# Zero fills on a DMA-bound kernel: 64 rows of 16 KB in place of 128 rows of 8 KB

## Chip, cores, metric

One core of a Trainium2 chip runs the whole program. The metric is the device time of one execution in microseconds; medians of several runs are quoted, with the lowest and highest. The time before is 646.59 us (646.42 to 647.03, 3 runs).

## The reference, cut to what matters

The program is the forward and backward pass of one decoder step for a single token: adaptive layer norm, attention over the last 4096 entries of a 65,536-entry cache, a gated feed-forward block, and the gradients of all inputs. What matters here is the size of two of those gradients:

```python
k = jnp.repeat(k_cache[:, :, Sk - W:, :], rep, axis=1)     # W = 4096 of Sk = 65536
v = jnp.repeat(v_cache[:, :, Sk - W:, :], rep, axis=1)
...
_out, _vjp = jax.vjp(_f, A_x, A_k_cache, A_v_cache, A_wq, A_wo, ...)
_grads = _vjp(grad_out)        # the gradients of k_cache and v_cache have the caches' shape
```

Only the last 4096 entries of each cache are read, so 15/16 of these two gradients (126 MB of bf16) is zero and has to be written all the same.

## The kernel before

The zeros are written to HBM, the chip's main memory, by 120 DMAs of 1 MiB ("fills") from one tile of zeros, 128 rows (partitions) of SBUF, the on-chip memory. They are filler: tuned lists say how many are issued after which step, so that the DMA engines always have work. Fills issued by GpSimd read bf16 zeros and write them as float32, so half as many bytes are read as are written ("widening"); the zeros that land are the same. Fills issued by ScalarE, in the feed-forward stage, read as much as they write.

```python
ZW = 4096
zeros = vt([P, ZW], "zeros", BF16)                     # 128 rows of 8 KB
nc.vector.memset(zeros.bitcast(U32), 0)
zregions = []
for og in (out_2, out_3):                              # gradients of k_cache, v_cache
    for g in range(G):
        region = og[0, g, 0:SKW, :].rearrange("r d -> (r d)").rearrange("(p x) -> p x", p=P)
        for i in range(region.shape[1] // ZW):
            zregions.append(region[:, i * ZW:(i + 1) * ZW])     # 128 rows of 8 KB, 120 KiB apart
zleft = list(zregions)
zeros8 = zeros[:, 0:ZW // 2]                           # 4 KB of each of the 128 rows

def zero(n, after=None, q=None):
    for _ in range(n):
        if not zleft:
            return
        if q is None:
            ins = nc.gpsimd.dma_start(out=zleft.pop(0).bitcast(FP32), in_=zeros8[:, :])   # widening
        else:
            ins = q.dma_start(out=zleft.pop(0), in_=zeros[:, :])
        ...
```

Three queues feed the same 16 DMA engines. GpSimd's queue (q0 in the profile) carries the 61 widening fills, 54 stores of gradients, and 14 loads of the feed-forward stage; SyncE's (q1) carries nearly all other loads and 7 large stores; ScalarE's (q10) carries the other 59 fills. Of the 61, 29 are issued before the feed-forward stage, among loads only. The last 32 come after it, and there the same queue carries stores.

```python
outer_dve(wq_t[j], h1[:, j:j + 1], dq_b)
nc.gpsimd.dma_start(out=dwq_view[:, j, :], in_=wq_t[j])    # a plain store: reads all 128 rows
zero(Z_DWQ[i])                                             # widening fills, same queue
```

Of the kernel before, what the change touches and what calls it, by code (L numbers as in the profile page):

```python
# [10 lines left out]
P = 128  # L11
FP32 = mybir.dt.float32
# [14 lines left out]
DH = 128  # L27
# [28 lines left out]
def kernel(  # L56
# [26 lines left out]
    nc = tc.nc  # L83
    SKW = A_k_cache.shape[2] - W
# [15 lines left out]
    def vt(shape, name, dt=FP32):  # L100
        return pool.tile(shape, dt, name=name)
# [4 lines left out]
    ZW = 4096  # L106
    zeros = vt([P, ZW], "zeros", BF16)
# [11 lines left out]
    zregions = []  # L119
    for og in (out_2, out_3):  # L120
        for g in range(G):
            region = og[0, g, 0:SKW, :].rearrange("r d -> (r d)").rearrange("(p x) -> p x", p=P)
            for i in range(region.shape[1] // ZW):
                zregions.append(region[:, i * ZW:(i + 1) * ZW])
    zleft = list(zregions)
    zeros8 = zeros[:, 0:ZW // 2]

    def dep(later, earlier):
        tc.add_manual_dep(later.ins, earlier.ins.name,
                          mybir.DependencyInfo(mybir.DependencyClass.Sync, mybir.DependencyReason.DATA),  # L130
                          reason="pace")

    def zero(n, after=None, q=None):
        for _ in range(n):
            if not zleft:
                return
            if q is None:
                ins = nc.gpsimd.dma_start(out=zleft.pop(0).bitcast(FP32), in_=zeros8[:, :])  # L138
            else:
                ins = q.dma_start(out=zleft.pop(0), in_=zeros[:, :])  # L140
            if after is not None:
                dep(ins, after)

# [104 lines left out]
    for j in range(KD):  # L248
        nc.sync.dma_start(out=wq_t[j], in_=wq_view[:, j, :])

    zero(Z_INIT)

    tp0 = ptp.tile([P, 24], BF16, name="tp_rows", tag="tp")
# [26 lines left out]
    for j in range(KD):  # L280
        for k in range(KM):
            mm = nc.tensor.matmul(mod_ps[:, k:k + 1], lhsT=wm_t[j][:, k * P:(k + 1) * P],
                                  rhs=cs_bf[:, j:j + 1], start=(j == 0 and k == 0), stop=(j == KD - 1),
                                  skip_group_check=True)
        if j < KD - 1:
            make_w01(j)
        zero(Z_MOD[j], mm)
# [25 lines left out]
    for j in range(KD):  # L313
        for h in range(HQ):
            mm = nc.tensor.matmul(q_ps[:, h:h + 1], lhsT=wq_t[j][:, h * P:(h + 1) * P],  # L315
                                  rhs=h1_bf[:, j:j + 1], start=(j == 0 and h == 0), stop=(j == KD - 1),
                                  skip_group_check=True)
        zero(Z_Q[j], mm)
# [429 lines left out]
```

## Time and profile before

| | before |
|---|---|
| median of 3 runs | 646.59 us |
| profiled span | 643.5 us |
| HBM read, written | 76.55 MB, 185.60 MB |
| GpSimd fills | 61, 7808 packets of 8 KB |

The page of a profile has a row of DMA shares (tenths, one digit for each fortieth of the span), a row of GB/s for the same slices, and a line for each queue (packets, MB, share of the 16 engines' time). The prediction below shows these lines of the kernel before. One more view of it is needed later, the windows of the closing stage, where stores and fills share q0. Its columns are the stretch and its length, busy time (and instructions) of each engine, the granted TensorE clock, the DMA share, and the GB/s moved.

```profile
core 0: us, PE busy (x) PEld busy (x) DVE busy (x) ACT busy (x) POOL busy (x), PEclk, DMA share, GB/s
492.00:544.00 52.00, 0.00 (x0) 0.00 (x0) 25.91 (x13) 0.00 (x0) 6.28 (x12) 0.50 1.10 425
544.00:634.00 90.00, 25.61 (x200) 20.41 (x199) 73.01 (x72) 33.75 (x56) 19.64 (x35) 0.50 1.07 423
```

The DMA share, 1.10 and 1.07, is over 1: the times of the packets overlap. In both stretches the engines move 423 to 425 GB/s, the plateau of this kernel.

### The profile page before, as it was taken

Reading aid. Unit: us, or ns where it says so; the run is one execution under the profiler, and the core shown is the slowest. Engines: PE = TensorE matmul, PEld = TensorE weight load, DVE = VectorE, ACT = ScalarE, POOL = GpSimd, SP = SyncE. Lnnn points to the kernel's source line nnn. Section 1 sums busy time; section 2 is a strip of 40 time slices with the busy share of each in tenths; the row PEclk is TensorE's granted clock in tenths of the full one; section 3 lists DMA queues with packets and bytes.
Section 4 is the critical chain, followed back from the end, with each engine's and each line's share of the span. In section 5 each row is a group of like instructions: output and inputs, shape, how many; then the busy total and the mean of one; then the engine's idle time right before and its main releaser. Section 6 shows DMA issues by size and latency. Waiting matters only on the chain.

```text
span 643.5 us, 7106 instructions
## 1 busy us (share of the span) xinstructions
PE 149.8 (23%) x2784; PEld 127.3 (20%) x2784; DVE 319.7 (50%) x626; ACT 206.8 (32%) x306; POOL 83.0 (13%) x137
## 2 busy tenths in 40 slices
PE   3122227562302020020201102310680000424300
PEld 2122215462301020010101101210460000423200
DVE  3442005600844518064180914899800079997194
ACT  2000016610531412543024432789670000425800
POOL 2000000040010100102001010212111012212211
PEclk9999999855555555555555555565755555555555
DMA  9999999999999999999999999999999999999996
GB/s 348 421 425 420 421 420 416 402 411 398 410 422 422 420 414 400 410 398 406 413 368 401 409 416 418 394 382 425 422 423 427 423 424 426 428 426 416 425 426 250
DMA packets 43810, 262.63 MB, mean 408 GB/s; under 512 B 4096, under 2 KB 4096, under 8 KB 18432
## 3 DMA queue, kind: packets, MB, share of 16 engines
q0 software_dynamic: 23184, 131.08, 51.5%
q1 hardware_dynamic: 12048, 69.22, 29.0%
q10 hardware_dynamic: 8544, 61.88, 23.8%
q8 instruction: 22, 0.36, 0.2%
q14 instruction: 12, 0.10, 0.0%
HBM read 76.55 MB, written 185.60 MB: 407 GB/s over the span
## 4 chain that ended last, share of the span: by engine, by line
DMA 64%; DVE 14%; ACT 11%; PE 5%; issue 4%; POOL 1%; SPq 0%; POOLq 0%; ACTq 0%; DVEq 0%
DMA out_dram<-arena 26%; DMA arena<-in_B_w_gate_dram 15%; DVE arena L172 7%; DMA arena<-in_w_mod_dram 7%; DMA arena<-in_A_wq_dram 6%; ACT arena L176 5%; DMA arena<-in_A_k_cache_dram 5%; DMA out_dram<-zeros 4%; DVE junk L172 2%; PE tp_kv L346 2%; DVE arena L168 1%; ACT arena L349 1%; ACT arena L234 1%; PE gu_ps L480 1%; ACT du_b L512 1%
## 5 line engine op out<-in xcount | busy, mean ns | idle before, releaser
L172 DVE CUSTOM_DVE_ANT_0 arena<-arena 128x4096 bf16<-128x4096 bf16 (+1 forms) x24 | 80.1, 3352 | 51.3 <-DMA arena<-in_w_mod_dram 51.3
L480 PE MATMUL gu_ps<-h_bf,arena 128*128 128x1 bf16 x448 | 16.8, 172 | 186.2 <-DMA arena<-in_B_w_up_dram 122.1
L155 DVE TENSOR_TENSOR hh<-sg,gu_ps 128x4 f32<-128x4 f32 x7 | 1.1, 158 | 113.8 <-ACT om L485 113.8
L138 POOL DMA_DIRECT2D out_dram<-zeros x61 | 33.7, 557 | 183.1 <-PE q_ps L315 49.5
L480 PEld LDWEIGHTS <-arena 128*128 128x128 bf16 x448 | 16.2, 118 | 187.9 <-issue 138.7
L653 PEld LDWEIGHTS <-arena 8*128 8x128 bf16 x256 | 25.9, 131 | 102.8 <-issue 99.2
L176 ACT ACTIVATE arena<-du_b,h 128x512 bf16<-128x512 bf16 x56 | 35.2, 711 | 33.8 <-DMA arena<-in_B_w_down_dram 31.3
L176 ACT ACTIVATE arena<-dg_b,h 128x512 bf16<-128x512 bf16 x56 | 35.3, 707 | 25.6 <-DMA out_dram<-zeros 12.7
L349 ACT COPY arena<-tp_kv 128x1024 bf16<-128x1024 bf16 x13 | 13.1, 1010 | 89.6 <-PE tp_kv L346 89.6
L657 ACT CAST arena<-ps_kv 128x512 bf16<-128x512 f32 x32 | 16.1, 691 | 75.1 <-DMA out_dram<-arena 75.1
L172 DVE CUSTOM_DVE_ANT_0 junk<-arena,b1k 128x1024 bf16<-128x1024 bf16 x28 | 34.2, 1223 | 8.2 <-DMA arena<-in_B_w_down_dram 7.7
L172 DVE CUSTOM_DVE_ANT_0 arena<-arena,b1k 128x1024 bf16<-128x1024 bf16 x32 | 36.7, 1218 | 0.4 <-ACT b1k L234 0.4
L172 DVE CUSTOM_DVE_ANT_0 arena<-arena,du_b 128x512 bf16<-128x512 bf16 x56 | 34.9, 686 | 3.5 <-ACT du_b L512 3.5
L172 DVE CUSTOM_DVE_ANT_0 arena<-arena,dg_b 128x512 bf16<-128x512 bf16 x56 | 34.8, 684 | 0.0
L653 PE MATMUL ps_kv<-DO_hd,arena 8*128 8x128 bf16 x128 | 15.9, 296 | 75.1 <-ACT arena L657 75.1
L176 ACT ACTIVATE arena<-b1k,o_col 128x1024 bf16<-128x1024 bf16 x32 | 33.4, 1137 | 0.0
L164 DVE COPY arena<-tp_kv 128x1024 bf16<-128x1024 bf16 x19 | 12.9, 690 | 27.3 <-PE tp_kv L346 27.2
L346 PE MATMUL tp_kv<-ident_bf,arena 128*128 128x128 bf16 x256 | 21.3, 246 | 20.7 <-DMA arena<-in_A_k_cache_dram 12.6
L484 ACT ACTIVATE sg<-gu_ps 128x4 f32<-128x4 f32 x7 | 1.2, 174 | 73.6 <-PE gu_ps L480 73.6
L433 POOL DMA_DIRECT2D arena<-in_B_w_up_dram x7 | 6.2, 891 | 131.3 <-DMA out_dram<-arena 102.3
L659 ACT ACTIVATE arena<-ps_kv 128x512 bf16<-128x512 f32 x32 | 16.1, 624 | 21.6 <-DMA out_dram<-arena 21.6
L346 PEld LDWEIGHTS <-arena 128*128 128x128 bf16 x256 | 18.4, 111 | 23.6 <-DMA arena<-in_A_k_cache_dram 13.5
(185 smaller groups left out, 377.5 us busy)
## 6 DMA issues: line engine op xcount, KB each, us to landing
out_dram<-zeros POOLq DMA_DIRECT2D x61, 1024.0 KB, 20.9
out_dram<-zeros ACTq DMA_DIRECT2D x59, 1024.0 KB, 21.4
out_dram<-arena POOLq DMA_DIRECT2D x46, 1024.0 KB, 20.2
arena<-in_A_wq_dram SPq DMA_DIRECT2D x16, 1024.0 KB, 20.7
arena<-in_w_mod_dram SPq DMA_DIRECT2D x8, 1536.0 KB, 30.8
arena<-in_A_wo_dram SPq DMA_DIRECT2D x8, 1024.0 KB, 23.7
arena<-in_w_mod_dram SPq DMA_DIRECT2D x8, 1024.0 KB, 27.3
arena<-in_B_w_down_dram SPq DMA_DIRECT2D x7, 1024.0 KB, 11.8
```

Of the source, the lines that this page charges most:

```text
L138: ins = nc.gpsimd.dma_start(out=zleft.pop(0).bitcast(FP32), in_=zeros8[:, :])
L164: return nc.vector.tensor_copy(out=out, in_=a)
L168: return nc.vector.tensor_scalar(out=out, in0=a, scalar1=s1, scalar2=None, op0=op0)
L172: return nc.vector.tensor_tensor_reduce(out=out, in0=w, in1=b, scale=1.0, scalar=0.0, op0=ALU.mult, op1=ALU.add, accum_out=acc)
L176: return nc.scalar.activation(out=out, in_=b, func=ACT.Copy, scale=col)
L234: last = nc.scalar.copy(out=o, in_=ps[:, :])
L346: nc.tensor.transpose(tp[:, t8 * P:(t8 + 1) * P], src[:, g, t_ * DH:(t_ + 1) * DH], ident_bf[:, :])
L349: last = nc.scalar.copy(out=o, in_=tp[:, :])
L480: nc.tensor.matmul(gu[:, half * 4 + jj:half * 4 + jj + 1], lhsT=w[:, j, jj::4], rhs=h2_bf[:, j:j + 1], start=(j == 0), stop=(j == KD - 1))
L653: nc.tensor.matmul(ps[:, t4 * DH:(t4 + 1) * DH], lhsT=rows[32 * g:32 * g + HG, t_ * P:(t_ + 1) * P], rhs=hd[32 * g:32 * g + HG, :], start= ...
L657: nc.scalar.copy(out=o, in_=ps[:, :])
L659: nc.scalar.activation(out=o, in_=ps[:, :], func=ACT.Copy, scale=float(scale))
```

## The change

The intent is to halve the number of packets of the widening fills: 64 rows of 16 KB written in place of 128 rows of 8 KB. For that each fill region becomes one contiguous MiB (for ScalarE's fills too, which keep 128 rows of 8 KB).

```diff
-            region = og[0, g, 0:SKW, :].rearrange("r d -> (r d)").rearrange("(p x) -> p x", p=P)
-            for i in range(region.shape[1] // ZW):
-                zregions.append(region[:, i * ZW:(i + 1) * ZW])
+            region = og[0, g, 0:SKW, :].rearrange("r d -> (r d)")
+            for i in range(SKW * DH // (P * ZW)):
+                zregions.append(region[i * P * ZW:(i + 1) * P * ZW])
 zleft = list(zregions)
-zeros8 = zeros[:, 0:ZW // 2]
+zeros8 = zeros[0:64, :]
 ...
-                ins = nc.gpsimd.dma_start(out=zleft.pop(0).bitcast(FP32), in_=zeros8[:, :])
+                ins = nc.gpsimd.dma_start(out=zleft.pop(0).rearrange("(p x) -> p x", p=64).bitcast(FP32), in_=zeros8[:, :])
             else:
-                ins = q.dma_start(out=zleft.pop(0), in_=zeros[:, :])
+                ins = q.dma_start(out=zleft.pop(0).rearrange("(p x) -> p x", p=P), in_=zeros[:, :])
```

So the change has three parts: the packets (16 KB), the addresses in HBM (contiguous), and the rows of SBUF that are read (0 to 63 only).

## The prediction

> **What bounds the kernel now.** I read the page first: the span, the row of DMA shares, the queues and the chain that ended last.
>
> ```profile
> span 643.5 us, 7106 instructions
> ...
> DMA  9999999999999999999999999999999999999996
> GB/s 348 421 425 420 421 420 416 402 411 398 410 422 422 420 414 400 410 398 406 413 368 401 409 416 418 394 382 425 422 423 427 423 424 426 428 426 416 425 426 250
> DMA packets 43810, 262.63 MB, mean 408 GB/s; under 512 B 4096, under 2 KB 4096, under 8 KB 18432
> ...
> q0 software_dynamic: 23184, 131.08, 51.5%
> q1 hardware_dynamic: 12048, 69.22, 29.0%
> q10 hardware_dynamic: 8544, 61.88, 23.8%
> ...
> DMA 64%; DVE 14%; ACT 11%; PE 5%; issue 4%; POOL 1%; SPq 0%; POOLq 0%; ACTq 0%; DVEq 0%
> ```
>
> The DMA engines are 90% busy or more in 39 of 40 slices; no compute engine passes 50%. The kernel is bound by DMA throughput: 262 MB at a plateau of about 427 GB/s would take 614 us, so only some 30 us are lost, at the head, in the middle stage with 1 KB rows, and at the tail. The chain agrees: 64% DMA. Queue q0 is what GpSimd issues (widening fills, its stores and some loads), q1 is SyncE, q10 is ScalarE. The list of DMA issues says what the change can touch:
>
> ```profile
> out_dram<-zeros POOLq DMA_DIRECT2D x61, 1024.0 KB, 20.9
> out_dram<-zeros ACTq DMA_DIRECT2D x59, 1024.0 KB, 21.4
> ```
>
> There are 120 fills of 1 MiB, nearly half of all bytes. The 61 from GpSimd read bf16 and write float32, so each reads half of what it writes; the 59 from ScalarE do not widen. A fill takes 21 us to land because it waits behind others, not because it is slow.
>
> Then I asked for the rate in stretches where the trace's DMA packets have one size or one mixture:
>
> ```profile
> core 0: us, PE busy (x) PEld busy (x) DVE busy (x) ACT busy (x) POOL busy (x), PEclk, DMA share, GB/s
> 20.00:30.00 10.00, 2.87 (x96) 2.71 (x96) 4.87 (x4) 0.00 (x0) 0.53 (x1) 1.00 1.07 420
> 124.00:150.00 26.00, 14.57 (x416) 13.85 (x415) 4.17 (x10) 4.38 (x6) 6.97 (x11) 0.63 1.13 410
> 168.00:176.00 8.00, 2.15 (x44) 1.99 (x41) 7.32 (x25) 4.96 (x7) 0.00 (x0) 0.50 1.12 427
> 630.00:633.00 3.00, 0.00 (x0) 0.00 (x0) 3.00 (x6) 0.00 (x0) 1.05 (x2) 0.50 1.02 411
> ```
>
> The last column is what matters. At 168 to 176 us nearly all packets are fills of 8 KB: 427 GB/s. At 630 to 633 all are plain stores of 4 KB: 411. At 20 to 30 the fills alternate with 12 KB weight loads: 420.
>
> Last I read the late part of the chain, because the wait there opens the closing stretch:
>
> ```profile
> 471.93 26.83 DMA out_dram<-arena
> 498.76 0.02 SPq L602
> ...
> 499.23 18.68 DMA arena<-in_w_mod_dram
> 517.92 0.02 issue
> 517.94 4.42 DVE arena L172
> ```
>
> VectorE has nothing to do from 467 to 518 us: it waits for a load on q1 that could start only when a store on q0 had landed. Both share the engines with fills.
>
> [...]With 12 KB loads on q1, the 8 KB fills of q0 carry about 40% of the bytes (8 of 20); with 2 KB loads (124 to 150 us) 78 to 80% (8 of 10); with 8 KB loads (503 to 518 us) 46 to 54%. [...]plain packets last 84 ns for 2 KB, 159 for 4 KB, 309 for 8 KB, so about 9 ns are fixed. The widening fills mostly last 322 alone and 341 when packets overlap; the 427 GB/s above corresponds to one per 307 ns per engine. [...]Here contiguous stores of 8 KB a row (gradients of k, v and wq) run at 426 to 428 in the late stage; 16 KB a row is not seen before.
>
> **The change part by part.**
>
> *Packets.* Each of the 61 widening fills becomes 64 packets of 16 KB: 7808 packets become 3904. From the windows: a 4 KB packet costs 4096 x 16 / 411 = 159.5 ns of an engine, an 8 KB packet 8192 x 16 / 427 = 307.0 ns. On a straight line through both, 16 KB cost 602 ns against 614 for two of 8 KB. Saved: 12 ns x 3904 / 16 engines = 2.9 us. That is an upper estimate: beside another queue part of the gap is probably already covered, and the 12 KB loads, at 420 to 422, are not faster than the 8 KB ones. I take 2 us.
>
> *Issue.* GpSimd spends 532 ns to issue a fill[...]. Nothing on the path.
>
> *Instructions.* No order changes: the comparison of the two programs finds the same rows on PE, VectorE, ScalarE and SyncE, and on GpSimd only the fills' shape differs.
>
> *Addresses.* All fills, ScalarE's too, now cover a contiguous 1 MiB instead of rows at a pitch of 120 KiB. Contiguous stores already reach 427, as the old pitch does: I count 0, with 2 us either way for the middle stage, where fills stand beside stores of 1 KB rows and the rate dips to about 330 for a few us at a time.
>
> *Shares.* [...]Fills are filler, and loads on q1 are waited for. In the first 100 us the fills are paced by matmuls that wait for these loads, so about one more fill gets ahead of a load, and the total before any point stays nearly the same. At 499 to 518 us q0 moved about half of 18.7 us x 424 GB/s, some 4 MB, and went on until about 526 us with another 1.2 MB. With 67% it would get those before the load lands: 1.2 / 0.424 = 2.8 us later. Against it, the store that lands at 498.8 waits behind fills on its own queue, which now drain faster. Net 0 to 2.8 us; I take 1.5 us lost.
>
> *Sum.* -2 + 1.5 + 0 = -0.5 us: 646.59 becomes about 646.
>
> **Rivals.**
>
> [...]A fill must read 512 KiB. [...]Against it: fills mostly alternate with loads, which read no SBUF[...]. Only at 166 to 176, 497 to 502 and in parts of 430 to 440 and 590 to 615 us does q0 run alone. I expect 0 to 4 us.
>
> *Fewer engines.* If 64 rows landed on 8 engines only, those would carry 8 MB of fills each and 12.4 MB of the rest: 20.4 MB at 26.7 GB/s per engine is 764 us. [...]
>
> *Better packets than thought.* If the widening itself costs a fixed 13 ns (322 against 309) that is now paid once for 16 KB, another 3 us go: 641 us. Overlap of packets (DMA share 1.12) speaks against it: that latency is already hidden.
>
> *Contiguity helps the middle stage.* If the dips there came from the fills' pitch, up to 8 us could go: 638 us. The dips come when the 1 KB-row stores end, so I think them theirs.
>
> **Range and chances.** The terms are all small beside 2% (13 us), and partly cancel. Centre 646 us. Low end 639: both kinder rivals in part. High end 657[...]. Under 633.7 would need an effect that I can't name: 4%. Above 659.5[...]: 14%. Within 2%: 82%.
>
> **What would show each step.** Queue q0 should have about 3900 packets fewer and the same bytes; its 16 KB packets should last 620 to 650 ns. [...]fills with double landing time and a DMA share near one half on average, fewer engines. The share step shows in the bytes of q0 against q1 at 10 to 30 and 503 to 518 us, and in when the w_mod load that VectorE waits for lands (517.9 us before). Addresses show on q10 alone: its 8 KB packets at 309 to 313 ns and the dips in the middle stage. The prediction is wrong if [...]small shifts of loads open idle stretches in the closing 120 us.

Passages of the prediction that say something of the hardware which no trace or run of this case shows are cut, and marked. -2 us (packets) + 1.5 (shares) + 0 (addresses) came to -0.5 us, 646 us. The 67% under "Shares" is the author's estimate from the shares of bytes in the trace before: where 8 KB fills stood beside 12 KB loads they had 40% (8 of 20), beside 8 KB loads 46 to 54%, so 16 KB fills beside 8 KB loads were given 16 of 24. The first rival: that the reads of SBUF from rows 0 to 63 become the bound. Its 0 to 4 us, and with it the high end of 657 us and the 14% for over 659.5, were estimates, shown by no trace.

Numbers of the trace before for what the prediction says without them: GpSimd's 129 transfers all land in the order of their issue, and its fills 20.9 us after it in the median, where 1 MiB at 427 GB/s takes 2.46 us, so a fill waits behind others. Before fills of the first 100 us GpSimd sat idle for 49.5 and 22.6 us until matmuls (into q_ps and mod_ps) had ended. The dip to about 330 is 331 GB/s at 334 to 342 us, after a store of 1 KB rows landed at 333.7.

## The result, and the profile after

The changed kernel takes 667.93 us (666.96 to 680.47, 3 runs; the slowest counts as a slow run, one over 1.5% above the fastest). Ratios in this document are the mean time of one kernel's fast runs over the mean of the other's fast runs of the same rounds, so they are not quite the ratio of the medians; here it is 1.032, with a 95% interval of 1.029 to 1.035. The prediction's range ended at 657.

The page of the changed kernel, for the lines shown of before:

```profile
span 666.2 us, 7106 instructions
...
GB/s 347 424 424 426 420 426 411 413 410 395 417 414 407 418 416 331 422 411 408 396 372 419 355 419 404 371 403 382 412 419 419 427 403 393 377 409 328 355 380 186
DMA packets 39906, 262.63 MB, mean 394 GB/s; under 512 B 4096, under 2 KB 4096, under 8 KB 18432
...
q0 software_dynamic: 19280, 131.08, 50.4%
q1 hardware_dynamic: 12048, 69.22, 26.9%
q10 hardware_dynamic: 8544, 61.88, 23.1%
...
DMA 70%; DVE 13%; ACT 6%; PE 5%; issue 3%; ACTq 1%; SPq 0%; POOL 0%; POOLq 0%; DVEq 0%
```

The bytes are the same and q0 has exactly 3904 packets fewer. The row of GB/s shows where the time went: the last eight slices but the very last were between 416 and 428 before, and now lie between 328 and 409. The queues' shares of the engines' time did not rise (q0 51.5 to 50.4%, q1 29.0 to 26.9, q10 23.8 to 23.1), so the shares alone would show nothing.

The windows of the changed kernel, at the stretches used in the prediction and in its closing stage (shifted with its milestones):

```profile
20.00:30.00 10.00, 1.44 (x48) 1.36 (x48) 2.45 (x2) 0.00 (x0) 0.00 (x0) 1.00 1.07 427
124.00:150.00 26.00, 13.83 (x392) 13.11 (x391) 4.09 (x10) 4.30 (x6) 7.50 (x12) 0.63 1.08 418
168.00:176.00 8.00, 2.83 (x69) 2.67 (x66) 7.33 (x21) 4.38 (x6) 0.00 (x0) 0.50 1.06 428
...
500.00:552.00 52.00, 0.00 (x0) 0.00 (x0) 19.87 (x10) 0.00 (x0) 6.17 (x12) 0.50 1.03 416
552.00:653.00 101.00, 25.60 (x200) 20.38 (x199) 78.78 (x73) 33.76 (x56) 19.35 (x36) 0.50 1.00 374
```

Where fills stand beside loads, the rate even rose (420 to 427, 410 to 418). Where fills run alone it stayed (427, 428). Where they share the queue with stores, it fell from 423 to 374 GB/s, while the DMA share still reads 1.00. Two more windows of the changed kernel part this further: from 604 to 642 us, where fills and stores move and no loads, and from 480 to 500 us, where loads carry about three tenths of the bytes beside them:

```profile
604.00:642.00 38.00, 9.57 (x72) 7.49 (x71) 16.17 (x26) 17.68 (x24) 7.63 (x13) 0.50 1.01 363
480.00:500.00 20.00, 5.15 (x43) 4.16 (x41) 0.00 (x0) 4.52 (x10) 3.59 (x7) 0.50 1.06 420
```

Last, the part of the chain of waits that answers to the one shown of before:

```profile
479.87 28.33 DMA out_dram<-arena
...
508.25 0.33 SPq L602
...
508.67 23.33 DMA arena<-in_w_mod_dram
532.02 4.43 DVE arena L172
```

VectorE's load now lands at 532.0 instead of 517.9 us. The milestones split the 22.7 us of the two profiled spans: 4.9 by the end of the feed-forward stage (409.9 to 414.8), 3.0 more by the issue of the last w_o store (471.9 to 479.9), 6.1 more by that load, and 8.6 after it. Not all of this is the loss that is to be explained: run e1 below, which keeps the change but for the rows, is later than before by 2.8, 3.2 and 6.7 us at the same three points and by 3.7 at the end (one profiled run each). Against e1 the changed kernel is later by 2.1, 4.8, 7.4 and 19.0 us, so more than half of that comes after the load.

Two other records of the trace bear on the slow stretch. A large DMA leaves 16 completion records; for GpSimd's transfers that ended between 560 and 640 us the median time from the first record to the last was 4.6 us before and is 8.4 now. The packet records of q0 show slow packets in the 90 us from 544 (before) and from 552 (after): of the 8 KB packets, which normally last 309 to 342 ns, 2 of 4162 lasted over 500 ns before, and 173 of 2404 do now; of the 16 KB fills, normally 624 to 642 ns, 110 of 768 last over 900. The slow ones last 616 and 1138 ns in the median, so these packets run at about half their rate. What spreads the completions is not shown: the records name no engine.

### The profile page after: what moved, and what is told of

It is laid out like the page before. It is cut to its first block, busy times and chain, and to the rows that moved or that the text cites. A ratio compares the mean times of both kernels' runs of the same rounds, so it can differ in the third digit from the quotient of the medians.

```text
span 666.2 us, 7106 instructions
## 1 busy us (share of the span) xinstructions
PE 150.4 (23%) x2784; PEld 127.5 (19%) x2784; DVE 319.6 (48%) x626; ACT 207.1 (31%) x306; POOL 83.2 (12%) x137
## 3 DMA queue, kind: packets, MB, share of 16 engines
q0 software_dynamic: 19280, 131.08, 50.4%
q1 hardware_dynamic: 12048, 69.22, 26.9%
q10 hardware_dynamic: 8544, 61.88, 23.1%
## 4 chain that ended last, share of the span: by engine, by line
DMA 70%; DVE 13%; ACT 6%; PE 5%; issue 3%; ACTq 1%; SPq 0%; POOL 0%; POOLq 0%; DVEq 0%
DMA out_dram<-arena 28%; DMA arena<-in_B_w_gate_dram 14%; DMA arena<-in_w_mod_dram 8%; DMA arena<-in_A_wo_dram 6%; DVE arena L172 6%; DMA arena<-in_A_wq_dram 5%; DMA arena<-in_A_k_cache_dram 5%; DMA out_dram<-zeros 3%; DVE junk L172 2%; DMA out_dram<-dx_orow 1%; PE gu_ps L480 1%; ACT arena L176 1%; DVE arena L168 1%; PE tp_kv L346 1%; ACT du_b L512 1%
```

## The experiments

Theory A, a supposition before these runs: reads of rows 0 to 63 alone, or of rows 64 to 127 alone, have a lower limit than reads of rows 32 to 95 or of all rows, and at this limit the fills collide with other reads. Rivals: B, the 16 KB packets take too large a share beside loads and stores; C, the contiguous addresses; D, something particular to the low rows. In the expectations, A1 is the form of A in which fills collide with fills, and A2 the form in which they collide with plain stores. Where the expectations explained A by parts of the hardware that no run here shows, the words are cut, and marked. All 12 runs computed correct results. Each call of four kernels shared its runs of the kernel before: medians 646.83 (first four), 646.76 (second), 646.62 (third). Medians and ranges in the table are over all runs, the ratios over fast runs alone; slow runs were one of three of the changed kernel, one of four of e2, two of four of e6 and three of four of e7.

| run | rows read by GpSimd fills | packet | bytes read of those written | median us (range) | ratio (95%) |
|---|---|---|---|---|---|
| before | 0-127 | 8 KB | 1/2 | 646.6 | 1 |
| after | 0-63 | 16 KB | 1/2 | 667.93 (666.96-680.47) | 1.032 (1.029-1.035) |
| e1 | 32-95 | 16 KB | 1/2 | 648.88 (647.14-650.77) | 1.003 (1.000-1.006) |
| e2 | 0-63, old addresses | 8 KB | 1/2 | 677.0 (670.0-684.17) | 1.042 (1.036-1.049) |
| e3 | 0-127, new addresses | 8 KB | 1/2 | 647.32 (645.56-648.4) | 1.000 (0.997-1.003) |
| e4 | 64-127 | 16 KB | 1/2 | 661.47 (658.06-662.36) | 1.021 (1.017-1.025) |
| e5 | 0-63 early, 32-95 late | 16 KB | 1/2 | 647.72 (646.8-650.42) | 1.002 (0.999-1.006) |
| e6 | 32-95 early, 0-63 late | 16 KB | 1/2 | 673.76 (664.88-681.93) | 1.033 (1.027-1.039) |
| e7 | 0-63 | 8 KB | 1 | 787.07 (769.22-802.82) | none given |
| e8 | 32-95 | 8 KB | 1 | 652.38 (650.9-653.07) | 1.008 (1.006-1.011) |
| e9 | 0-63 | 16 KB | 1/4 | 648.35 (646.13-652.16) | 1.003 (0.999-1.007) |
| e10 | 0-127, old addresses | 8 KB | 1/4 | 646.66 (645.6-648.63) | 1.000 (0.998-1.002) |
| e11 | 0, 2, 4 ... 126 | 16 KB | 1/2 | 648.81 (646.05-649.38) | 1.002 (0.999-1.005) |
| e12 | 0-63 and 64-127 in turn | 16 KB | 1/2 | 655.45 (653.65-660.04) | 1.014 (1.010-1.018) |

### Which part of the change: e1 to e4

e1 keeps the packets and the addresses and moves the rows that are read:

```diff
-zeros8 = zeros[0:64, :]
+zeros8 = zeros[32:96, :]
```

> The changed kernel with one edit: the fills read rows 32 to 95 of the zeros instead of 0 to 63; packets (16 KB), addresses and order stay. Theory A ([...]fills collide there with plain stores): [...]643 to 648 us, ratio to before 0.995 to 1.003, and the late stage back at 420 GB/s or more. Rival B (16 KB packets take too large a share in turn with loads and stores): still 664 to 670 us, 1.03. Rival C (contiguous addresses in HBM): still 1.03.

Measured: 648.88 us, just above the range expected, 1.003. Nearly the whole loss is gone with a change of rows, so neither the packet size nor the addresses suffice to cause it. The last part of the closing stage, which was to be back at 420 GB/s or more, is at 414:

```profile
552.00:637.00 85.00, 25.37 (x200) 20.18 (x197) 71.92 (x71) 32.88 (x55) 18.61 (x34) 0.50 1.02 414
```

A gap of 4 us accounts for most of that: from 588 to 592 us the DMA share is 0.51 (213 GB/s), and on either side of it the rate is 426 and 421. The changed kernel has such a gap too (595 to 605 us, share 0.73), so its 374 GB/s is not all slow packets.

e2 goes the other way: the kernel before with its addresses and its 8 KB packets, read from rows 0 to 63:

```diff
-zeros8 = zeros[:, 0:ZW // 2]
+zeros8 = zeros[0:64, :].rearrange("p (h x) -> p h x", h=2)
-  out=zleft.pop(0).bitcast(FP32), in_=zeros8[:, :]
+  out=zleft.pop(0).bitcast(FP32).rearrange("(h p) x -> p h x", h=2), in_=zeros8
```

> The kernel before with one edit: the GpSimd fills keep their addresses and 8 KB packets but read them from rows 0 to 63, two packets a row. Theory A[...]: about as slow as the changed kernel, 660 to 672 us, ratio 1.02 to 1.04. Rivals B (packet size) and C (addresses): neither is touched, so 646 to 648 us, 1.00.

Measured: 677.0 us, 1.042, worse than expected. The rows alone bring the loss. That they bring more of it with 8 KB packets than the whole change did (1.032, and the intervals do not overlap) is not explained.

e3 changes only the addresses:

```diff
-zeros8 = zeros[0:64, :]
+zeros8 = zeros[:, 0:ZW // 2]
-  out=zleft.pop(0).rearrange("(p x) -> p x", p=64).bitcast(FP32)
+  out=zleft.pop(0).rearrange("(p x) -> p x", p=P).bitcast(FP32)
```

> Only the addresses of the change: every fill writes a contiguous MiB, with 128 rows of 8 KB from all rows of the zeros. Theories A and B: 644 to 649 us, ratio 0.997 to 1.004. Rival C (addresses): 660 us or more; if the addresses cost the few us that the middle stage lost, 649 to 652.

Measured: 647.32 us, 1.000. The addresses cost nothing.

e4 takes the other half:

```diff
-zeros8 = zeros[0:64, :]
+zeros8 = zeros[64:128, :]
```

> The changed kernel with the fills read from rows 64 to 127. Theory A[...]: as slow as the changed kernel, 662 to 672 us, ratio 1.025 to 1.04. Rival D (something particular to rows 0 to 63, such as another user of the low rows): 644 to 650 us, 1.00.

Measured: 661.47 us, 1.021, just under the range expected (and, at a threshold of 2%, not clear of it). The upper half loses too, so rival D falls as the main cause; that it loses a third less than the lower half is not explained by these runs.

### Where it happens: e5 and e6

Both read rows 0 to 63 for one part of the 61 fills, and rows 32 to 95, found harmless, for the rest:

```diff
+                lo = 0 if (len(zleft) > 91) else 32      # e5: the 29 early fills; e6: <= 91, the 32 late ones
-                  in_=zeros8[:, :]
+                  in_=zeros[lo:lo + 64, :]
```

> Rows 0 to 63 only for the 29 GpSimd fills before the feed-forward stage, where q0 and q1 carry loads and fills but no stores; the 32 later ones read rows 32 to 95. Theory A2 (the loss needs fills beside plain stores[...]): 645 to 651 us, ratio 1.000 to 1.006. Rival A1[...]: about half of the loss, 654 to 660 us, ratio 1.012 to 1.02.

> The opposite: rows 32 to 95 for the 29 early fills, rows 0 to 63 for the 32 after the feed-forward stage, which share q0 with plain stores. Theory A2: nearly the whole loss, 661 to 670 us, ratio 1.022 to 1.036, with the spread between the first and the last of a transfer's 16 completion records at 8 us or more after 560 us. Rival A1: about half of it, 654 to 660 us.

Measured: e5 647.72 us, 1.002; e6 673.76 us, 1.033. Rows 0 to 63 cost nothing that can be resolved where fills stand beside loads or run alone, early in the program, and the loss arises in the late stage, where the stores are. No run took the stores away, so their part rests on the stage and on what moves in it. I sorted the closing stage, from 436 us to the ends of the windows shown, into slices of 2 us by the packet records: in slices without loads in which fills and stores both move, the rate is 378 GB/s in the changed kernel and 380 in e6, against 426 in e1 and in e5; in slices in which loads are over a third of the bytes, it is 413 and 398 against 421 and 424. Slices with over nine tenths of fills are at 407 and 400 against 429 in both, so the slowing in the late stage is not confined to the slices in which both move. The windows of the closing stage, first of e5 and then of e6 (last column GB/s, before it the DMA share):

```profile
552.00:635.00 83.00, 25.34 (x199) 20.12 (x197) 71.00 (x65) 32.84 (x55) 18.73 (x33) 0.50 1.03 425
```

```profile
552.00:655.00 103.00, 25.61 (x200) 20.39 (x199) 79.45 (x68) 33.75 (x56) 21.13 (x38) 0.50 0.97 370
```

The instructions are the same, and the rate is 425 in one and 370 in the other. In the completion records of GpSimd's transfers from 560 to 640 us the spread is 4.5 us in e5 and 9.2 in e6, and of the 16 KB packets in these windows (727 and 772) none lasts over 900 ns in e5 but 83 do in e6.

### The limit of these rows by itself: e7 and e8

To see the limit without widening, these fills read the full MiB: each row's 8 KB is read twice.

```diff
+  out=zleft.pop(0).rearrange("(p h x) -> p h x", p=64, h=2),
+  in_=zeros[0:64, :].unsqueeze(1).broadcast_to([64, 2, ZW])      # e8: zeros[32:96, :]
```

> [...]the GpSimd fills do not widen but read 8 KB of each of rows 0 to 63 twice, so each reads the full MiB[...]; packets 8 KB. Theory A[...]: where such fills run alone, near 168 to 176 us, the rate falls to 190 to 225 GB/s and packets last about 600 ns; in all 690 to 780 us. If [...]: packets at 309 to 342 ns there and 645 to 675 us.

> The control of the run above: not widening, read twice from rows 32 to 95[...]. Theory A: 8 KB packets at 309 to 342 ns, 645 to 655 us, ratio 0.998 to 1.012. If reading twice or not widening costs by itself, it is slow as well, 660 us or more.

Measured: e7 787 us (769 to 803; three of its four runs, the profiled one among them, count as slow and no ratio is given; the plain quotient of the medians is 1.22), e8 652.38 us, 1.008. In e7 the stretch in which such fills run alone came at 184 to 190 us. Windows of e7, of that stretch and of the stretch in which the fills alternate with 2 KB loads:

```profile
184.00:190.00 6.00, 2.06 (x40) 1.98 (x40) 5.46 (x17) 4.76 (x6) 0.00 (x0) 0.50 0.98 208
128.00:160.00 32.00, 12.10 (x352) 11.79 (x352) 2.52 (x8) 2.08 (x4) 7.25 (x11) 0.57 1.01 260
```

Windows of e8, beside the same loads and then nearly alone (about a tenth of its packets are 8 KB loads):

```profile
128.00:150.00 22.00, 12.57 (x384) 12.05 (x384) 1.93 (x6) 2.03 (x3) 7.71 (x12) 0.56 1.02 421
168.00:176.00 8.00, 2.06 (x40) 1.98 (x40) 7.36 (x25) 5.66 (x8) 0.00 (x0) 0.50 1.01 425
```

The same transfer runs at 208 GB/s from rows 0 to 63 and at 425 from rows 32 to 95; its 8 KB packets last 628 ns in the one and 309 in most of the other. That is half, to 2%: the lower limit that theory A supposed, measured. (Half of the 427 GB/s of the kernel before is 214, and twice its 309 ns is 618; the expected 190 to 225 GB/s and about 600 ns stand around these.) That e7's profile is of a slow run does not explain it: its one fast run took 769 us, far above all others too. The 0.8% that e8 loses bounds what reading all bytes instead of half is worth; e1, which reads half from the same rows in 16 KB packets, loses 0.3%.

### How much must be read, and in which order: e9 to e12

e9 reads a quarter (1 byte widened to 4), from rows 0 to 63:

```diff
-  in_=zeros8[:, :]
+  in_=zeros[0:64, 0:ZW // 2].bitcast(mybir.dt.uint8)
```

> The changed kernel, rows 0 to 63 and 16 KB packets, but widening from 1 byte to 4, so that a fill reads a quarter of what it writes. Theory A2: [...]the loss shrinks, to between a quarter and two thirds of the 21 us: 651 to 661 us, ratio 1.007 to 1.022. Rival (rows 0 to 63 are bad however little is read): 664 us or more. If the reading threshold is sharp: 645 to 649.

Measured: 648.35 us, 1.003. The loss did not shrink in proportion; it is gone. My expectation of a graded loss was wrong, and its last branch, 645 to 649 us, held. At half the bytes the fills, at full rate, ask for about all that rows 0 to 63 deliver: e7 read 208 GB/s from them, and the changed kernel's fills alone, at 428 GB/s written, read 214. At a quarter they would read 107 at that rate, so by this estimate they leave half of it free.

e10, a candidate, does the same in the kernel before, with 128 rows:

```diff
-zeros8 = zeros[:, 0:ZW // 2]
+zeros8 = zeros[:, 0:ZW // 4].bitcast(mybir.dt.uint8)
```

> A candidate: the kernel before with the widening fills reading 1 byte for 4 written, 128 rows of 8 KB. Reading the full MiB instead of half cost 0.8% in the plain run against before; if that comes from the read bytes, a quarter gains another 0 to 0.4%: 644 to 647 us. If a quarter brings nothing, or the conversion is slower: 646 to 652.

Measured: 646.66 us, 1.000. Reading less than half brings no more, so no version here beats the kernel before.

e11 reads every second row:

```diff
-zeros8 = zeros[0:64, :]
+zeros8 = zeros[0:128:2, :]
```

> The changed kernel, 64 rows of 16 KB from rows 0, 2, 4 to 126. [...] 645 to 650 us, ratio 0.998 to 1.006. [...]652 to 668, ratio 1.01 to 1.03.

Measured: 648.81 us, 1.002. That is in the first of the two ranges, which stood for no loss from these rows (the second, for a loss). At the resolution of these runs, not the number of 64 rows is the trouble, but which rows they are.

e12 alternates between the two halves from fill to fill:

```diff
+                lo = 64 * (len(zleft) % 2)
-                  in_=zeros8[:, :]
+                  in_=zeros[lo:lo + 64, :]
```

> The changed kernel with rows 0 to 63 and 64 to 127 in turn from fill to fill. Theory with a lasting lead[...]: turns cancel the lead, 647 to 655 us, and the spread of completions after 560 us under 7 us. If each single meeting of a fill with a store costs its time at once: 660 to 670 us, as the two runs with one half.

Measured: 655.45 us, 1.014, with a spread of completions of 5.9 us from 560 to 640 us. That is just outside the first expectation and below either half alone (1.021 and 1.032). So turns take back a part of the loss. The lead in the expectation was supposition; that two fills in flight, one from each half of the rows, hold each other up less fits as well. The run shows neither.

## Why the prediction was wrong

**The bound** was read rightly: DMA throughput, 262 MB at a plateau near 427 GB/s. The bytes stayed the same, and the loss is a lower rate, mostly in the closing stage (423 to 374 GB/s).

**The step that failed** is the size of the first rival, that the reads of SBUF become the bound, put at 0 to 4 us with the words "fills mostly alternate with loads, which read no SBUF" and "Only at 166 to 176, 497 to 502 and in parts of 430 to 440 and 590 to 615 us does q0 run alone". It looked for harm where fills meet fills. Early in the program there is none: 428 GB/s in the first of these stretches, and e5 loses nothing that can be resolved. It passed over that q0 itself carries plain stores in the closing stage, though it lists them, that these read all 128 rows of their tiles, and that fills meet stores there. By their ratios the result and e6 (1.032 and 1.033) put the late fills at the whole loss, 21 us. The prediction had named this sign itself, the limit binding in mixed stretches too. With the rate that e7 measured, 208 GB/s, the 512 KiB that a fill reads take 2.52 us by my estimate, against 2.46 us for its writing at 427 GB/s: about hidden and with nothing to spare, which is what the fills alone showed (428).

**The kind of reckoning behind it** also failed. It compared average demand with capacity. By that account even a mixture about fits: a fill reads half of what it writes, all of it from rows 0 to 63, and a plain store reads half of its bytes from these rows, so at 427 GB/s either asks 214 GB/s of them, by estimate, where e7 read 208. What the records show instead is completions that spread (8.4 us between first and last in place of 4.6) and some packets at about half rate (616 ns in place of 309 to 342). With slack the loss is gone (e9, 1.003), and with turns it is less (e12, 1.014). The spread alone is not the loss: e1 shows spreads of about 9 us (GpSimd's transfers) between 420 and 560 us without losing time there to speak of. So the step that failed is shown, and how a fill and a store hold each other up is not: the trace does not tell which engine a packet ran on.

**Packets.** 3904 fewer, and 624 to 642 ns each, as forecast (620 to 650). The saving of 2 us is not resolved: fills alone went from 427 to 428 GB/s where the straight line promised 435, and of the 7 and 8 GB/s that two mixed stretches gained, e1 has 1 and 7 (421 and 417 GB/s in the same windows). One reading of the prediction was off: in the stretch where fills run alone, 341 ns is the commonest duration of an 8 KB fill packet, not 322.

**Issue.** Nothing on the path, as said. The median issue went from 532 to 537 ns.

**Shares.** Right in kind: the packet records put q0 at 50 to 58% of the bytes at 8 to 30 us (40% before). With 2 KB loads it had 77% before (130 to 150 us), a little under the 78 to 80 that the prediction read. In e1, which has the large packets and not the loss of rows 0 to 63, VectorE's load landed at 524.6 us, 6.7 later than before and more than the 0 to 2.8 that the prediction gave, but 3.0 of it was regained by the end. The large packets need not be its cause: e10, with the packets of before, landed it at 523.4, and the load took 22.1 us there as it took 22.3 in e1 (18.7 before). The net of packets and shares is e1's 0.3%, not told from zero.

**Addresses.** 0, as counted (e3). **Fewer engines** and **contiguity** as rivals: refuted, by 428 GB/s with fills alone and by e3.

## What to carry to other kernels

Before giving a transfer fewer rows, measure at which rate those rows are read, and ask what else reads SBUF while it runs: here fills from rows 32 to 95 ran at 425 GB/s (e8) and the same fills from rows 0 to 63 at 208 (e7). Judge DMA by GB/s, not by its busy share, which read 1.00 at 374 GB/s; the spread of completions is a hint, but e1 had a wide one without the loss. And when a margin is "just enough" on average, look for the stage in which two users of it meet, on the same queue too.
